# An S5 scan beside a Mish layer: row statistics of the last block on ScalarE, and another order of four w2 pairs

## The chip, the core and the metric

The kernel runs on one NeuronCore of a Trainium2 chip. The metric is the device time of one execution in microseconds (us), lower is better. TensorE (PE) multiplies matrices into PSUM banks, VectorE (DVE) and ScalarE (ACT) work element by element on SBUF and PSUM, GpSimd (POOL) and SyncE (SP) mostly issue DMAs here. Every engine works through its own list in order; where an instruction needs another engine or a DMA it waits on a semaphore, and everything behind it on that engine waits too.

## The reference

```python
x  = A_x                                   # 2048 x 1024
xn = (x - mean(x)) / sqrt(var(x) + eps)    # over the 1024 columns of each row
# A: diagonal state space model, complex
Bu = xn @ B_bar.T ;  h[t] = Lam_bar * h[t-1] + Bu[t]
yA = 2 * real(h @ Cmat.T) + xn * Dskip
# B: dense layer, F = 3584
hB = xn @ w1 + b1 ;  yB = (hB * tanh(softplus(hB))) @ w2      # Mish
out = x + yA + yB
```

## The kernel before

The 2048 rows are done in four blocks of 512 (blk 0 to 3). Each block has a first part, the products of xn with w1 (1024 x 3584) and with B, and a second, "dense 2" (Mish values times w2) followed by the product of the scanned states with C. The results of dense 2 and of C collect in the eight PSUM banks, and `finish` (L1676 in the first two blocks, L1679 in the last two) adds them to x.

In the third and fourth block (and in part in the second) the products are done by Strassen's scheme with seven products instead of eight. It needs sums of pieces of the operands. The pieces of w2 are scaled on ScalarE (`d2_row`, L1279), summed on VectorE (one `k` step is one sum, L1297), and each piece is stored by GpSimd to the scratch tensor `w2d` in HBM (`d2_store`, L1269). SyncE loads them back into the ring (`ring<-w2d`, L481), a set of seven slots of 512 KB in SBUF through which all streamed operands go to TensorE; a slot is free again when TensorE has used it. The rows of w2 go through this in five groups of two tile pairs; a group has four sums, and one semaphore counts the stores of its first three. A ring load of any of these three pieces waits for all three stores.

The Strassen products of dense 2 are called `D` (a step `D70` is product 7, first half of the rows; 10 matmuls) and `X`. Four pairs of w2 tiles go in plainly (`pl24`, `pl10`, `pl12`, `pl26`). `t0`, `t1`, `t2` and `ta0` are sums of Mish values on VectorE (L1399), `t0` for `D7`, `ta0` for `X3`. `G` steps scale Mish values on ScalarE (L938), `g` steps are Mish itself (L931), `kp` steps put PSUM results aside (L1618 on VectorE, L1624 on ScalarE).

The layer norm of the next block is made during the present one. `E` is the mean and variance of 128 rows on VectorE, `lr` the square root on ScalarE, `li` its inverse on VectorE, `ns` the normalised rows on ScalarE (L640), `tr` the transposing DMA into `xnT` (L653), `sk` and `sx` what VectorE makes from them for the next block (L647, L649, L1514). A second way stands in the code, and the second block uses it for the third: `st` (two passes on ScalarE that sum up as they go) and `nr` (root on ScalarE, two small instructions on VectorE).

```python
def ln_stats_only(blk, q):                 # E
    for h in range(2): vop(... e.bn_stats(stats[:, s, h, :], xx[...512 columns]))      # L595
    vop(... e.bn_aggr(mv[:, q, :], stats[:, s, :, :]))                                 # L597
def next_stats(blk, q):                    # st
    aop(... e.activation(xn[:, q, :], x, AF.Copy, accum_out=lnq(0, q)))                # L617
    aop(... e.activation(lnq(1, q), lnq(0, q), AF.Copy, scale=-1.0 / D))               # L619
    aop(... e.activation(xn[:, q, :], x, AF.Square, bias=lnq(1, q), accum_out=lnq(2, q)))  # L621
def next_root():                           # nr
    aop(... e.activation(ln[:, 3, :], ln[:, 2, :], AF.Sqrt, scale=1.0 / D, bias=kon[:, 2:3]))  # L625
    vop(... e.reciprocal(ln[:, 3, :], ln[:, 3, :]))                                    # L627
    vop(... e.tensor_tensor(ln[:, 4, :], ln[:, 1, :], ln[:, 3, :], op=ALU.mult))       # L628
```

The order of the work is written out by hand: one string of step names for each block (`FIRST`, `WHOLE`, `STEPS`, `LAST`), from left to right. `STEPS` is the third block. A step puts its instructions at the end of the lists of the engines that it uses. In the strings `a` to `d` with a digit are Strassen products with B, `p` to `z` those with w1, and an `e` before such a name is their evacuation from PSUM; `r` turns the states by their phases (L947, L953, L955), `sc` is a scan (L1406), `to` and `so` turn back, `al` scales the scanned states (L1650), `h16` to `h19` scale the rows of the last group of w2, `l0` loads the next x, `m4` a raw piece of w2, `Y` and `Q` are the product with C, `fin` is `finish`.

`W2_ORDER` is the order in which the first and the second block load the fourteen pairs of w2 tiles and use them in dense 2 (steps `da0` to `da27` of `WHOLE`, two for each pair). At the end of the second block's dense 2 two steps, `m2` and `m3`, load raw pieces of w2 over Mish values that are used up: `m2` first into tiles 20 to 23 of `act`, then into 24 to 27. These DMAs stand in GpSimd's list, and each waits until TensorE is done with its tiles. `h8` to `h15` scale these pieces, and four sums (`kd0`) that wait for their stores stand in VectorE's list ahead of the second block's `finish`.

Of the kernel before, what the change touches and what calls it, by code (L numbers as in the profile page):

```python
# [142 lines left out]
def bass_parallel_sum__ssm_conv_s5__dense_activation_mish__prompt_kernel(  # L143
    nc: bass.Bass,
    A_x: bass.AP,
    A_Lambda_re: bass.AP,
    A_Lambda_im: bass.AP,
    A_B_re: bass.AP,
    A_B_im: bass.AP,
    A_C_re: bass.AP,  # L150
    A_C_im: bass.AP,
    A_log_dt: bass.AP,
    A_Dskip: bass.AP,
    B_x: bass.AP,
    B_w1: bass.AP,
    B_b1: bass.AP,
    B_w2: bass.AP,
    out: bass.AP,
):
    build_kernel(nc, A_x, A_Lambda_re, A_Lambda_im, A_B_re, A_B_im, A_C_re, A_C_im,  # L160
                 A_log_dt, A_Dskip, B_w1, B_b1, B_w2, out)


def build_kernel(nc, A_x, A_Lambda_re, A_Lambda_im, A_B_re, A_B_im, A_C_re, A_C_im,
# [19 lines left out]
    GROUPS = ((0, 7), (7, NPL), (NPL, NPL + 8), (NPL + 8, NF), (12, 16), (16, 20), (20, 24), (24, 28))  # L184
    TILES = [*range(12)]
    NFG = {2: 5, 3: GF}
    W2_ORDER = tuple(range(14))
    EARLY, LATE = ((0, 20),), ((20, 28),)
    PLAIN = [(f, f + 1) for f in (24, 10, 12, 26)]
    PASSING = {}  # L190
# [19 lines left out]
    STEPS = ("p1 p5 ep1 ep5 p2 ep2 k0 k0 q1 eq1 p3 k0 q5 p6 q2 k0 ep6 eq2 s1 eq5 O0 k0 ep3 p7 es1 O0 ep7 s5 es5 k0 O0 q6 eq6 s2 es2 O0 p4 ep4 k0 q7 eq7 s6 "  # L210
# [8 lines left out]
    LAST = ("p1 ep1 p5 ep5 p2 ep2 q1 eq1 q5 eq5 p6 ep6 q2 eq2 s1 es1 p7 ep7 s5 es5 p3 ep3 q6 eq6 s2 es2 M5 p4 ep4 q7 eq7 q3 eq3 k0 k0 s6 es6 q4 eq4 g0 K0 "  # L219
# [223 lines left out]
    for blk in range(NB):  # L443
# [7 lines left out]
        else:  # L451
            items += [("w2", g) for g in W2_ORDER]
        items += [("c", j) for j in range(NJ)] if blk >= FAST else []
# [853 lines left out]
    def row_sizes(g):  # L1307
        s = (NF // 2 + g) % NRING
        for j in range(2):
            r = 2 * W2_ORDER[g] + j  # L1310
            src = ring[:, s, j * D:(j + 1) * D]
# [3 lines left out]
    def late_sizes(g, s):  # L1315
        for j in range(2):
            r = 2 * W2_ORDER[g] + j
            src = ring[:, s, j * D:(j + 1) * D].rearrange("p (d t) -> p d t", d=2)
            aop(lambda e, src=src, r=r: e.activation(CT[:, 0:2, 1, TB:D], src, AF.Abs, accum_out=wp[:, r:r + 1]),
                reads=[b_ring[s]], writes=[b_snap[0], b_wp])  # L1320
# [207 lines left out]
    def perform(blk):  # L1528
# [10 lines left out]
        for f0 in range(20, NF, 2) if blk == FAST else ():  # L1539
            left[at_item[blk, "w2", W2_ORDER[f0 // 2]]] += 1  # L1540

# [32 lines left out]
        def dense(f, us, chained=False):  # L1574
            g = (4 * REAL[f // 4] + f % 4) // 2 if split else f // 2
            at = at_item[blk, "w2", g]
            s = at % NRING
            assert n_item[0] <= at < n_loaded[0]
            wt = ring[:, s, :].rearrange("p (f d) -> p f d", f=2)
            for u in us:  # L1580
                q, h = u // 2, u % 2
                t, b_t = place(blk, f)
                opens = first[u]
                first[u] = False
                mm2(u, t[:, q * P:(q + 1) * P], wt[:, f % 2, h * TB:(h + 1) * TB], [b_t, b_ring[s]], at, opens=opens,
                    chained=chained, tell=f % 2 == 1 and u == us[-1])

        def in_order(n, us):
            dense(2 * W2_ORDER[n // 2] + n % 2, us)

        def sizes_of(g):
            at = at_item[blk, "w2", W2_ORDER[g]]
            late_sizes(g, at % NRING)
            if used(at):
                release()
# [279 lines left out]
```

## Time and profile before

| | us |
|---|---|
| median of 3 runs (lowest, highest) | 591.37 (590.75, 593.43) |
| the profiled execution | 591.81 |
| its span in the trace | 590.6 |
| TensorE busy in the span | 582.7 |
| VectorE, ScalarE, GpSimd busy | 511.2, 402.0, 151.9 |

The profiled execution took 591.81 us, 1.2 us more than its span, and lies 0.44 us above the median. Block boundaries by TensorE's first product with w1: the second block begins at about 161 us of the span, the third at 308, the fourth at 451. In the rows of the trace, the first number is the start, the second the time that a merged row takes, both in us, "xN" the number of instructions, and brackets give the idle time of the engine just before the row and what ended it.

### The profile page before, as it was taken

The page shows a single profiled execution, that of the slowest core. Times are in us where ns is not written, and L with a number is a line of the kernel's source. Part 1 is how long each engine was busy: PE and PEld are TensorE (multiplying, and loading weights), DVE is VectorE, ACT ScalarE, POOL GpSimd, SP SyncE. Part 2 cuts the span into 40 slices and gives each one's busy share as a digit, 9 for nine tenths or more (in the row PEclk, how much of TensorE's full clock was granted, in tenths as well). Part 3 has the DMA queues.
Part 4 walks back from the last instruction along what each step waited for, and adds up shares of the span by engine and source line. Part 5 has one row for each costly group of instructions (what it writes and reads, how often), then busy time and mean ns, then how long its engine had stood idle before and what let it go on. Part 6 is the DMA issues. An engine that isn't in the chain of part 4 may idle for free.

```text
span 590.6 us, 9767 instructions
## 1 busy us (share of the span) xinstructions
PE 582.7 (99%) x3631; PEld 353.0 (60%) x3631; DVE 511.2 (87%) x784; ACT 402.0 (68%) x541; POOL 151.9 (26%) x215
## 2 busy tenths in 40 slices
PE   9999999999999999999999999999999999999998
PEld 8644444444447887444448888644446888854444
DVE  6999999999796878998957789999997569789995
ACT  4859995489297778999636779976222788892330
POOL 2899200134424421332161243200000013100000
DMA  9999999999668987999999959998945946989832
GB/s 242 309 243 263 231 179 221 316 326 361 226 243 279 322 291 262 338 309 207 273 396 394 348 205 299 333 335 252 290 157 196 388 184 214 339 320 317 296 118 72
DMA packets 115369, 160.84 MB, mean 272 GB/s; under 512 B 55802, under 2 KB 66682, under 8 KB 115322
## 3 DMA queue, kind: packets, MB, share of 16 engines
q1 hardware_dynamic: 98512, 107.31, 60.6%
q0 software_dynamic: 13728, 45.62, 22.4%
q10 hardware_dynamic: 3082, 7.29, 3.4%
q8 instruction: 29, 0.48, 0.3%
q14 instruction: 18, 0.15, 0.1%
HBM read 114.05 MB, written 34.08 MB: 251 GB/s over the span
## 4 chain that ended last, share of the span: by engine, by line
PE 88%; DMA 5%; DVE 3%; ACT 3%; issue 1%; POOL 0%; DVEq 0%
PE ps L1544 44%; PE ps L1063 15%; PE ps L985 11%; PE ps L1755 10%; PE ps L1773 5%; DMA act<-in_B_w_dram 2%; DMA w2d<-act 1%; PE ps L713 1%; DMA ring<-w2d 1%; PE ps L722 1%; DMA w2d<-hb 1%; DVE xx L1676 1%; ACT act L1279 1%; ACT hb L1279 1%; PE ps L675 1%
## 5 line engine op out<-in xcount | busy, mean ns | idle before, releaser
L1544 PE MATMUL ps<-ring,act 128*128 128x512 bf16 (+1 forms) x716 | 156.2, 379 | 0.0
L1544 PEld LDWEIGHTS ps<-ring,act 128*128 128x128 bf16 (+1 forms) x716 | 70.0, 98 | 83.3 <-DMA ring<-w2d 0.2
L1544 PE MATMUL ps<-ring,hT 128*128 128x512 bf16 (+1 forms) x390 | 83.4, 376 | 0.0
L1083 ACT ACTIVATE snaps<-ps,par,cs 128x256 f32<-128x256 f32 x100 | 54.5, 562 | 40.8 <-PE ps L1063 38.5
L947 DVE TENSOR_TENSOR mt<-hT,tab 128x2048 bf16<-128x2048 bf16 (+1 forms) x56 | 68.0, 1214 | 0.4
L1544 PEld LDWEIGHTS ps<-ring,hT 128*128 128x128 bf16 x390 | 38.1, 98 | 45.0
L1406 DVE TENSOR_TENSOR_SCAN hT<-cs,qi,hT 128x512 bf16<-128x512 f32 x48 | 60.1, 1273 | 0.0
L1063 PE MATMUL ps<-TT,ring 128*128 128x256 f16 x480 | 59.8, 273 | 0.0
L1755 PE MATMUL ps<-xnT,ring 128*128 128x512 bf16 x264 | 57.3, 379 | 0.0
L1100 DVE SCALAR_TENSOR_TENSOR act<-ps,cs,snaps 128x512 bf16<-128x512 f32 x54 | 39.4, 747 | 16.0 <-PE ps L1063 13.9
L1063 PE MATMUL ps<-xnT,ring 128*128 128x256 bf16 x400 | 50.4, 273 | 1.4 <-DVE xx L1676 1.4
L1063 PEld LDWEIGHTS ps<-TT,ring 128*128 128x128 f16 (+1 forms) x480 | 46.8, 98 | 6.5
L1269 POOL DMA_DIRECT2D w2d<-hb x35 | 25.0, 716 | 87.4 <-ACT hb L1279 50.4
L1755 PEld LDWEIGHTS ps<-xnT,ring 128*128 128x128 bf16 x264 | 25.8, 98 | 31.0
L1063 PEld LDWEIGHTS ps<-xnT,ring 128*128 128x128 bf16 (+1 forms) x400 | 38.9, 98 | 6.8 <-issue 1.9
L1650 ACT ACTIVATE hT<-hT,wz 128x1024 bf16<-128x1024 bf16 x16 | 18.0, 1146 | 36.5 <-DVE hT L1646 36.5
L931 ACT ACTIVATE act<-act 128x2048 bf16<-128x2048 bf16 (+3 forms) x13 | 33.0, 2559 | 2.0 <-DVE act L1086 1.9
L1010 DVE TENSOR_TENSOR hT<-ps,snaps 128x512 f16<-128x512 f32 x36 | 23.8, 687 | 11.9 <-ACT snaps L1002 10.0
L938 ACT ACTIVATE act<-act,cs 128x512 bf16<-128x512 bf16 x48 | 30.8, 708 | 0.1
L1212 POOL DMA_DIRECT2D wsd<-hb x35 | 19.0, 546 | 42.2 <-DVE hb L1238 25.4
L1766 ACT ACTIVATE act<-ps,par 128x512 bf16<-128x512 f32 (+1 forms) x40 | 23.6, 660 | 8.2 <-PE ps L1755 8.2
L1223 ACT ACTIVATE hb<-hb,cs 128x2048 bf16<-128x2048 bf16 x10 | 19.4, 1995 | 14.1 <-DVE xx L1676 12.7
(237 smaller groups left out, 1038.2 us busy)
## 6 DMA issues: line engine op xcount, KB each, us to landing
ring<-wsd SPq DMA_DIRECT2D x110, 256.0 KB, 4.9
ring<-in_B_w_dram SPq DMA_DIRECT2D x52, 512.0 KB, 5.5
ring<-ctd SPq DMA_DIRECT2D x24, 512.0 KB, 4.6
ring<-w2d SPq DMA_DIRECT2D x24, 512.0 KB, 4.7
ring<-w2d SPq DMA_DIRECT2D x36, 256.0 KB, 4.6
wsd<-hb POOLq DMA_DIRECT2D x35, 256.0 KB, 4.8
w2d<-hb POOLq DMA_DIRECT2D x35, 256.0 KB, 5.1
hb<-in_B_w_dram POOLq DMA_DIRECT2D x20, 256.0 KB, 5.4
```

What stands on the lines that cost most here:

```text
L931: aop(lambda e: e.activation(t, t, AF.Mish), reads=b, writes=b)
L938: aop(lambda e, a=a, y=y: e.activation(a, a, AF.Copy, scale=y), reads=[b_a, b_y], writes=[b_a])
L947: vop(lambda e: e.tensor_tensor(mt[:], u.unsqueeze(1).to_broadcast([P, 2, 2, TB]), tab[:, :, j, :].unsqueeze(2).to_broadcast([P, 2, 2, TB] ...
L985: PE.mm(lambda e, w=w, x=x, o=o, begin=begin, end=end: e.matmul(ps[:, bank, o:o + TH], lhsT=w, rhs=x, start=opens and begin, stop=end, ski ...
L1063: PE.mm(lambda e, w=w, x=x, o=o, begin=begin, end=end: e.matmul(ps[:, bank, o:o + TH], lhsT=w, rhs=x, start=opens and begin, stop=end, ski ...
L1083: aop(lambda e, o=o, p=p, j=j: e.activation(o, p, AF.Identity, scale=ig, bias=b1(f0 + j)), reads=[b_ps[b], b_par, b_ig], writes=b_dst)
L1100: vop(lambda e: e.scalar_tensor_tensor(out=dst, in0=bank(b), scalar=ig, in1=src, op0=ALU.mult, op1=ALU.add), reads=[b_ps[b], b_snap[k], b_ ...
L1269: PO.dma(lambda e: e.dma_start(w2d[at // 4][:, at % 4 * TB:(at % 4 + 2) * TB].rearrange("p (j t) -> p j t", j=2), t[:, :, d, :]), sem, rea ...
L1406: vop(lambda e: e.tensor_tensor_scan(out=hT[:, ci, j, :], data0=cj("r", j).to_broadcast([P, TB]), data1=hT[:, ci, j, :], initial=init, op0 ...
L1544: PE.mm(lambda e: e.matmul(ps[:, bank, lo:hi], lhsT=lhsT, rhs=rhs, start=opens, stop=last, skip_group_check=split), reads=reads, writes=[b ...
L1755: PE.mm(lambda e, k=k, w=w: e.matmul(ps[:, bank, :], lhsT=w, rhs=xnT[:, k, :], start=k == 0, stop=k == NK - 1), reads=[b_ring[s]] + b_xnT, ...
L1773: PE.mm(lambda e, ci=ci, k=k: e.matmul(ps[:, bank + ci, :], lhsT=BT[:, ci, j, k, :], rhs=xnT[:, k, :], start=k == 0, stop=k == NK - 1), re ...
```

## The change

`W2_ORDER` becomes 0 to 9, 12, 10, 11, 13: in the first two blocks tiles 24 and 25 are used ahead of 20 to 23.

In the third block the four `E` steps, `lr0` and `li0` go, and `st0` to `st3` and `nr0` come in. Three of the `E` stood before dense 2, the fourth just after `t0`; the `st` stand among the `G` steps of dense 2 and after `kp3`, and `nr0` behind `to0`. Several neighbours change places in the same stretch.

```diff
-    W2_ORDER = tuple(range(14))
+    W2_ORDER = (*range(10), 12, 10, 11, 13)
...
-             "ec5 d5 ed5 d1 c6 k0 ed1 ec6 c3 ec3 d6 G0 ed6 G2 d3 c7 r1 ed3 ec7 l0 x1 h16 d7 ed7 x5 E1 ex1 h17 c4 h18 E0 x2 h19 ex2 ec4 k0 y5 d4 ex5 ed4 E2 "
-             "x6 ex6 y1 y2 ey1 ey5 k0 ey2 x7 x3 ex7 ex3 y6 r2 x4 ey6 k0 ex4 k0 z1 z5 ez1 G3 ez5 k0 z2 k0 y7 y3 ez2 k0 z6 z3 ez6 ey7 ez3 g2 D11 G7 ey3 y4 "
-             "k0 ey4 z7 ez7 G8 g6 G9 D10 z4 t0 D70 E3 ez4 G10 t1 kp2 t2 r3 r4 D71 D20 lr0 g7 G12 kp0 D21 r5 G4 G5 X5 li0 X6 r6 kp1 G11 kp3 pl24 ns2 pl10 "
-             "ns0 r7 ns1 G6 G13 tr0 ns3 tr1 tr2 tr3 pl12 pl26 sc20 sc00 sc21 sc50 sc01 sc10 to0 sc11 so0 al0 ta0 X3 to1 so1 sc30 al1 to2 sc41 sc31 so2 to3 "
...
+             "G1 k0 d1 c6 ec5 ed1 ec6 c3 ec3 d6 ed5 G0 ed6 d3 c7 r1 ec7 x1 ed3 h16 d7 x5 l0 h17 c4 ed7 h18 h19 ex1 x2 ex2 G2 ec4 k0 d4 ex5 y5 x6 ex6 y1 y2 "
+             "ed4 ey1 ey5 k0 x7 x3 k0 ex7 ey2 y6 ex3 r2 x4 ey6 ex4 k0 z1 k0 z5 z2 k0 ez1 y7 ez5 k0 y3 z6 ez2 G3 z3 ez6 ey7 ez3 ey3 D11 g2 G7 y4 k0 ey4 z7 "
+             "ez7 G8 D10 z4 g6 t0 D70 ez4 G9 G10 kp2 t1 D71 t2 r3 r4 D20 g7 G12 G4 D21 r5 kp0 X5 r6 G6 kp1 st1 G5 X6 G11 st2 kp3 G13 pl24 st0 sc01 sc21 "
+             "pl10 sc20 pl12 sc50 r7 sc00 st3 pl26 sc11 to0 nr0 sc10 ns1 so0 ta0 ns0 X3 to1 sc31 so1 tr0 sc30 ns3 al0 to2 ns2 sc41 al1 sc51 sc40 so2 to3 "
...
```

The lists of the engines show what this moves. First VectorE, late in the first part of the third block (one piece of the difference; L1297 are the sums of w2, L1100 and L1010 evacuations of products):

```order
-L595 BN_STATS stats<-xx 128x6 x2
-L597 BN_AGGR mv<-stats 128x2
-L595 BN_STATS stats<-xx 128x6 x2
-L597 BN_AGGR mv<-stats 128x2
-L1100 SCALAR_TENSOR_TENSOR act<-ps,cs,snaps 128x2x256
-L1297 TENSOR_TENSOR hb<-hb 128x2x512
-L595 BN_STATS stats<-xx 128x6 x2
-L597 BN_AGGR mv<-stats 128x2
-L1297 TENSOR_TENSOR hb<-hb 128x2x512
+L1100 SCALAR_TENSOR_TENSOR act<-ps,cs,snaps 128x2x256
+L1297 TENSOR_TENSOR hb<-hb 128x2x512 x3
 L1100 SCALAR_TENSOR_TENSOR act<-ps,cs,snaps 128x2x256 x3
```

The statistics are gone, and three sums instead of two stand ahead of the next three evacuations; of the five that followed these, four in a row are left, and a later single sum has moved up into that row.

Second ScalarE in dense 2, from its last group of scalings on (one piece of the difference):

```order
+L617 ACTIVATE xn,ln<-xx 128x1024
+L619 ACTIVATE ln<-ln 128x1
+L621 ACTIVATE xn,ln<-xx,ln 128x1024
 L1624 ACTIVATE KS<-ps,wz 128x512 x2
+L938 ACTIVATE act<-act,wz 128x512 x2
+L617 ACTIVATE xn,ln<-xx 128x1024
+L619 ACTIVATE ln<-ln 128x1
+L621 ACTIVATE xn,ln<-xx,ln 128x1024
+L617 ACTIVATE xn,ln<-xx 128x1024
+L619 ACTIVATE ln<-ln 128x1
+L621 ACTIVATE xn,ln<-xx,ln 128x1024
+L625 ACT_TABLE_LOAD
```

The piece begins with the second of the two `st` that now stand ahead of `kp3` (L1624); two more follow behind it, and the root with its table load comes after the last; before, two table loads and the root stood ahead of the last Mish group of the block.

Third VectorE at the end of dense 2, where the inverse root now stands (one piece of the difference):

```order
+L1406 SCALAR_TENSOR_TENSOR hT<-cs,qi,hT 128x512 x2
+L947 TENSOR_TENSOR mt<-hT,tab 128x2048
+L627 RECIPROCAL ln<-ln 128x4
+L628 TENSOR_TENSOR ln<-ln 128x4
 L1406 SCALAR_TENSOR_TENSOR hT<-cs,qi,hT 128x512
 L1644 TENSOR_TENSOR hT<-mt 128x512
```

L627 stands behind the first turn back (`to0`), one scan and `so0` ahead of `ta0`. On SyncE the four transposing DMAs go behind the first four of the eight loads of C; on GpSimd the load `m4` goes behind a second store. TensorE keeps its order but for two products with B and w1 that change places with neighbours, and but for the tiles of the new `W2_ORDER`.

6 rows, old and new, of the table STEPS are left out of this document.

## Prediction

> **What bounds the kernel now.** I read the page's first part, then TensorE's timeline for the places where it is idle, then the chain of work and each waiting engine's rows around those places. The page (engines: busy time, share, instructions):
>
> ```profile
> span 590.6 us, 9767 instructions
> PE 582.7 (99%) x3631; PEld 353.0 (60%) x3631; DVE 511.2 (87%) x784; ACT 402.0 (68%) x541; POOL 151.9 (26%) x215
> ```
>
> TensorE bounds the kernel; only 590.6 - 582.7 = 7.9 us of the span are left to win, and only where TensorE waits. Its timeline, the rows with idle time ahead of them in the part that the change touches, and the rows that date dense 2:
>
> ```profile
> 308.29 1.03 PE L1063 MATMUL ps<-xnT,ring 128*128 128x256 bf16 x8 [1.43 <-DVE xx L1676]
> ...
> 314.08 1.05 PE L1063 MATMUL ps<-TT,act 128*128 128x256 f16 x8 [1.27 <-DVE act L1238]
> ...
> 381.38 0.60 PE L1544 MATMUL ps<-ring,S 128*128 128x512 f16 x2
> 383.04 1.04 PE L1544 MATMUL ps<-ring,S 128*128 128x512 f16 x4 [1.06 <-DMA ring<-w2d]
> 384.94 3.19 PE L1544 MATMUL ps<-ring,S 128*128 128x512 f16 x14 [0.87 <-DMA ring<-w2d]
> 387.98 35.56 PE L1544 MATMUL ps<-ring,act 128*128 128x512 bf16 x164
> 423.37 27.79 PE L1544 MATMUL ps<-ring,hT 128*128 128x512 bf16 x128
> ```
>
> Two waits at the third block's start (1.43 + 1.27 = 2.70 us, on VectorE) and two in `D7` (1.06 + 0.87 = 1.93 us, on ring loads from `w2d`). Between 387.98 and the next block nothing waits: 164 matmuls fill 423.37 - 387.98 = 35.39 us, 0.216 each. The chain of work says what the waits hang on:
>
> ```profile
> 279.65 11.96 DMA act<-in_B_w_dram
> ...
> 297.07 6.91 DMA w2d<-act
> ...
> 307.01 4.53 DVE xx L1676 x4
> ...
> 373.10 0.61 DVE hb L1297
> ...
> 374.00 4.58 DMA w2d<-hb
> ...
> 378.61 6.29 DMA ring<-w2d
> 384.94 66.22 PE ps L1544 x306
> ```
>
> The first three: `m2`'s load, the stores of its pieces, the second block's `finish`. The last five: a w2 sum on VectorE, its store, the ring load that waited for it, `D7`.
>
> **The wait in D7.** SyncE's waits and issues, and its ring loads from 372 to 386 (count, size, median us to landing); then VectorE:
>
> ```profile
> SPq L481 <- DMA w2d<-hb: 4.8, 2, 3.5
> 375.61 0.32 SPq L481 DMA_DIRECT2D ring<-w2d  x1
> ...
> 381.87 0.39 SPq L481 DMA_DIRECT2D ring<-w2d  x1
> ring<-w2d SPq DMA_DIRECT2D x12, 256.0 KB, 5.5
> ```
>
> ```profile
> 363.16 1.41 DVE L595 BATCH_NORM_STATS2 stats<-xx 128x6 f32<-128x512 bf16 x2
> ...
> 365.78 2.07 DVE L1100 SCALAR_TENSOR_TENSOR act<-ps,cs,snaps 128x512 bf16<-128x512 f32 x3 [0.41 <-issue]
> ...
> 369.69 2.74 DVE L1297 TENSOR_TENSOR hb<-hb 128x1024 f16<-128x1024 bf16 x4
> ...
> 383.57 3.02 DVE L1399 TENSOR_TENSOR act<-act 128x2560 f16<-128x2560 bf16 x2 [0.16 <-ACT act L938]
> ```
>
> SyncE waited twice for stores, 3.5 and 1.3 us: at 375.61 for a group whose third sum is the first of the four at 369.69, and at 378.61 for the last group's third sum, at 373.10. Three `E` go ahead of these: at least 3 x 1.41 = 4.2 us of VectorE, by the row at 363.16. What is late next is not VectorE but the products it evacuates: the three L1100 at 365.78 keep their place behind TensorE's `x3`, so they hardly move. But the first group's third sum now stands ahead of them, with its store done long before the slot is free; its 3.5 us go. The last group's third sum becomes the fourth of the row of four instead of standing at 373.10. That row starts earlier by the 0.41 of idle time at most, at about 369.4, and the sum ends at 369.4 + 2.74 = 372.1 instead of 373.7, 1.6 earlier. Its ring load goes out at 378.61 - 1.6 = 377.0 and lands after 5.5 to 6.3 at 382.5 to 383.3; TensorE wants it at 381.38 + 6 x 0.216 = 382.7. Left: 0 to 0.6.
>
> The next in the row are the loads for `D20` behind them. The pair that holds its third unit needs the slot of the product that ends at 381.38; its second half goes out at 381.87 and by the median of 5.5 lands at 387.4. `D7` has 20 matmuls and 4 of `D20` come first: unhindered, TensorE asks for the pair at 381.38 + 24 x 0.216 = 386.6, where today it asks at 387.98 + 0.86 = 388.8. So up to 0.8 (1.6 if it takes the 6.29 of the row above) of the gain turns into a new wait there. The four loads ahead of it are spread over more time, so I take 0.5: a gain of 1.93 - 0.5 = **1.4 us**, ends 0.3 (a 1.6 wait left) and 1.93.
>
> The fourth `E` costs nothing today: the two `t1`, `t2` sums at 383.57 waited for ScalarE's L938, so VectorE would only have waited longer. Its removal gains nothing. `h16` to `h19` moved together, `m4` one store later, the two products that changed places: bounded by the same waits, 0, since TensorE had no wait between 314.08 and 381.38.
>
> **The new statistics.** ScalarE's rows (the second block's `st`, two starts of it; then dense 2):
>
> ```profile
> 241.69 1.04 ACT L617 ACTIVATE xn<-xx 128x1024 bf16<-128x1024 bf16 x1
> ...
> 244.25 1.04 ACT L617 ACTIVATE xn<-xx 128x1024 bf16<-128x1024 bf16 x1
> ...
> 381.00 2.54 ACT L938 ACTIVATE act<-act,cs 128x512 bf16<-128x512 bf16 x4
> ...
> 384.71 1.28 ACT L632 ACT_TABLE_LOAD   x1
> 386.00 0.30 ACT L632 ACTIVATE ln<-mv,kon 128x4 f32<-128x4 f32 x1
> ...
> 387.61 1.91 ACT L931 ACTIVATE act<-act 128x2048 bf16<-128x2048 bf16 x1
> ...
> 400.91 1.27 ACT L1624 ACTIVATE KS<-ps,wz 128x512 f32<-128x512 f32 x2 [6.35 <-PE ps L1544]
> ```
>
> One `st` takes 244.25 - 241.69 = 2.56 us. Without the root and its two loads, Mish starts at 384.7 instead of 387.61 and ends at 386.6; then five scaling pairs of 1.25 (2.54 for four instructions) and two `st`: 386.6 + 6.2 + 5.1 = 397.9. That fills the 6.35 us in which ScalarE waited for `X6`. `kp3` follows when `X6` ends, 400.9 - 1.4 = 399.5, and takes 1.2; then a scaling pair, two `st`, the load and the root: 399.5 + 1.2 + 1.25 + 5.1 + 1.28 + 0.3 = **408.6**.
>
> VectorE waits for that root at L627, and behind it stand a scan, `so0`, `ta0`, all turns and scans, and the third block's `finish`:
>
> ```profile
> 408.04 1.28 DVE L1406 TENSOR_TENSOR_SCAN hT<-cs,qi,hT 128x512 bf16<-128x512 f32 x1
> ...
> 409.89 1.48 DVE L1399 TENSOR_TENSOR act<-act 128x2560 f16<-128x2560 bf16 x1
> ...
> 446.02 1.28 DVE L1679 SCALAR_TENSOR_TENSOR xx<-ps,wz,KS 128x1024 bf16<-128x1024 f32 x1 [1.22 <-PE ps L1544]
> ```
>
> Up to L627 VectorE does what it did up to 408.04 (less `li0`, 0.3), so it comes there at about 407.7 and waits 0.9. With 0.3 for its two small instructions, 1.85 (409.89 - 408.04) for scan and `so0`, and 1.48, `ta0` ends at 408.6 + 0.3 + 1.85 + 1.48 = 412.2 instead of 411.4. TensorE reaches `X3` 40 matmuls ahead of 423.37, at 414.7, with the gain at 413.3. Margin 1.1: cost 0. `finish` had 1.22 us to spare, less 0.8 later and 1.4 earlier wanted: it runs 1.0 late against TensorE; but the fourth block's first product needs its first bank only 451.0 - 447.3 = 3.7 after it, so 0. I bound this term by 0 and 2 (root two or more us late, less margin).
>
> The Trainium skill, "ScalarE: Activation LUTs", section "What ACT_TABLE_LOAD costs", gives 1283 ns for the load and some 1380 ns more of drain at every switch. In the rows above the root starts 0.01 after a load of 1.28, with no such gap. By the page the root would come at 410.0, `ta0` would eat the margin and X3 would wait 0.3: 590.8 instead of the 590.5 below.
>
> The transposing DMAs wait on SyncE for the fourth slot of C, by TensorE's pace some 418 instead of 409; the sums that read `xnT` stand just ahead of `finish` at 446. That leaves over 20 us: 0.
>
> **The new w2 order.** In the second block tiles 20 to 23 are now done two tiles later. `m2`'s first load, which GpSimd issued as soon as tile 23 was done, waits 16 x 0.216 = 3.45 us longer; its second load waits for tile 27 as before. GpSimd's rows, the first load's size and time to land, and what GpSimd's queue moved in 273:276, 276:279 and 288:291 (packets, MB, share):
>
> ```profile
> 272.62 0.72 POOL L1264 DMA_DIRECT2D act<-in_B_w_dram  x1 [1.93 <-PE ps L1544]
> 279.65 2.14 POOL L1264 DMA_DIRECT2D act<-in_B_w_dram  x3 [6.32 <-PE ps L1544]
> act<-in_B_w_dram POOLq DMA_DIRECT2D x1, 512.0 KB, 10.5
> q0 software_dynamic: 7, 0.02, 7.9%
> q0 software_dynamic: 80, 0.31, 82.8%
> q0 software_dynamic: 131, 0.50, 44.0%
> ```
>
> Both loads must land before `h8`, at 291.6, and from there the chain above runs to TensorE without slack: `finish` is late already, TensorE waits 2.70. A load later by s costs s. In its first 3.4 us the load moved 0.02 MB, the next three 0.31. If all 0.31 are pushed behind 288, they take 0.31 / 0.50 x 3 = 1.9 us there; if the queue moves them a little later beside the same transposing DMAs, almost nothing. Ends: 3.45 lost (the whole wait) and, if the transposes get done sooner without it, 2.70 won. Nearest are the rows of its slow start: I take **0.5 us lost**. The first block only loads rows of B 3.45 later, in VectorE's and ScalarE's slack there: 0.
>
> **Sum.** 591.81 - 1.4 + 0.5 + 0 = 590.9 for the profiled execution, which lies 0.44 above the median: **590.5**, 0.9 less than before (0.15%). A change of this kernel under 0.5% (3.0 us) can hardly be told from none.
>
> **Rivals.**
> - Nothing won: the gain ends in the loads of `D20`, which need the slot freed at 381.38, and the rest in `m2`. 591.4. For it: the slot's date does not move. Against it: even the slowest of these loads leaves 0.3, and a load lost to `m2` must cost the rest.
> - Slower by `m2`: the 3.45 us are passed on whole. From 1.4 on, it decides the sign. 591.37 - 1.4 + 3.45 = 593.4. For it: the chain there has no slack. Against: 0.02 MB in the first 3.4 us.
> - Slower by the root: each 1 us after 409.7 at which L627 is released delays `X3` by 1 us, and after 411.1 the kernel is slower than with no change. Two `st` of 3.6 instead of 2.56 behind `kp3` would do that. 591.37 + 1 = 592.4.
> - Both waits shrink: `m2` lands sooner since the transposes are not shared with; up to 1.4 + 2.0: 588.0. For it only that engine time was held by the transposes.
>
> **How the numbers follow.** Forecast 0.52 (590.5, its own range 589.6 to 591.1), nothing won 0.22 (591.4), `m2` 0.12 (593.4), root 0.07 (592.4), both 0.07 (588.0). The range for 8 in 10 leaves out the farther half of "both" and most of the `m2` case: 588.8 to 592.8. Faster by over 0.5% (under 588.4) only in half of "both" and little else: 0.06; slower (over 594.3) by an `m2` load that costs more than 3.45 or a root late as well: 0.05; the rest 0.89.
>
> **What would show it.** The waits in `D7` on ring loads fall from 1.93 to 0.6 or less, a wait of 0 to 1 us appears some 5 us on, at `D20`. ScalarE has no idle time ahead of `kp3`; VectorE waits about 0.9 for ScalarE at L627, and no row of TensorE waits at `X3`. The two waits near 308 grow together by about 0.5. I am wrong if TensorE waits for L1399 at `X3`, for a product's evacuation around 362 to 367 (ScalarE's list is tight there, with `h16` to `h19` ahead), or if the waits near 308 change by more than 2.

## The result, and the profile after

The changed kernel takes 588.78 us (median of 9 runs, 587.50 to 589.71); the kernel before, timed beside it, 592.47 (9 runs, 590.29 to 596.26). The ratio is 0.9933, interval 0.9906 to 0.9959: 0.67% faster, where 0.15% was forecast. The profiled execution took 588.81 us with a span of 587.5. Two very slow runs do not enter the ratios further down: one of the kernel before at 1030.73 us, which is left out of the counts too, and one at 597.15 with the third block's steps alone.

```profile
span 587.5 us, 9776 instructions
PE 582.2 (99%) x3631; PEld 352.0 (60%) x3631; DVE 507.3 (86%) x772; ACT 411.1 (70%) x561; POOL 151.8 (26%) x215
```

The span is 3.1 us shorter (590.6 before). TensorE's timeline, its rows from the third block's start to the end of dense 2 that have idle time in brackets, and the two that stood at 308.29 and 314.08 before:

```profile
307.24 1.04 PE L1063 MATMUL ps<-xnT,ring 128*128 128x256 bf16 x8
...
311.61 1.04 PE L1063 MATMUL ps<-TT,act 128*128 128x256 f16 x8
...
378.89 4.48 PE L1544 MATMUL ps<-ring,S 128*128 128x512 f16 x20
...
385.30 1.02 PE L1544 MATMUL ps<-ring,act 128*128 128x512 bf16 x4 [1.06 <-DMA ring<-w2d]
386.62 33.84 PE L1544 MATMUL ps<-ring,act 128*128 128x512 bf16 x156 [0.30 <-DMA ring<-w2d]
420.30 27.79 PE L1544 MATMUL ps<-ring,hT 128*128 128x512 bf16 x128
```

Both waits at the third block's start are gone: 1.43 + 1.27 = 2.70 us. The 20 matmuls of `D7` (the row at 378.89) run without a wait, and `D20` behind them waits 1.06 + 0.30 = 1.36 instead of the 1.93 in `D7`: 0.57 less. Together 3.27 between the two profiles, of which the rest of the program gives back 0.2. So most of it comes from the place where I expected a loss of 0.5: `m2`. GpSimd's rows there, then ScalarE's first `h` step and VectorE's `kd0` and `finish`:

```profile
276.63 0.72 POOL L1264 DMA_DIRECT2D act<-in_B_w_dram  x1 [5.39 <-PE ps L1544]
280.20 2.14 POOL L1264 DMA_DIRECT2D act<-in_B_w_dram  x3 [2.86 <-PE ps L1544]
```

```profile
287.95 8.42 ACT L1279 ACTIVATE act<-act,cs 128x1024 bf16<-128x1024 bf16 x8 [0.49 <-DMA act<-in_B_w_dram]
```

```profile
298.59 2.94 DVE L1297 TENSOR_TENSOR act<-act 128x1024 f16<-128x1024 bf16 x4 [1.06 <-DMA w2d<-act]
302.27 1.22 DVE L1676 TENSOR_TENSOR xx<-ps,xx 128x1024 bf16<-128x1024 f32 x1 [0.74 <-PE ps L1544]
```

The same two steps before:

```profile
291.63 4.27 ACT L1279 ACTIVATE act<-act,cs 128x1024 bf16<-128x1024 bf16 x4 [4.72 <-DMA act<-in_B_w_dram]
```

```profile
304.06 2.94 DVE L1297 TENSOR_TENSOR act<-act 128x1024 f16<-128x1024 bf16 x4 [7.10 <-DMA w2d<-act]
```

The first load goes out 4.0 us later (276.63 against 272.62), and yet the data are there 3.7 us earlier (287.95 against 291.63). `kd0` starts at 298.59 instead of 304.06, and `finish` now waits for TensorE, not TensorE for `finish`. What the DMAs did in that stretch, in windows of 4 us (DMA share and GB/s are the last two columns), before:

```profile
276.00:280.00 4.00, 4.00 (x20) 1.83 (x19) 1.92 (x13) 3.88 (x7) 0.35 (x1) 1.00 1.20 139
280.00:284.00 4.00, 4.00 (x20) 1.78 (x19) 3.59 (x16) 4.00 (x3) 1.79 (x3) 1.00 0.99 187
284.00:288.00 4.00, 4.00 (x20) 1.84 (x19) 3.90 (x7) 2.91 (x2) 0.00 (x0) 1.00 1.02 119
```

and after:

```profile
276.00:280.00 4.00, 4.00 (x20) 1.80 (x19) 2.17 (x12) 3.85 (x9) 0.72 (x1) 1.00 1.12 210
280.00:284.00 4.00, 4.00 (x20) 1.82 (x19) 3.48 (x18) 4.00 (x3) 2.14 (x3) 1.00 1.06 365
284.00:288.00 4.00, 4.00 (x20) 1.79 (x19) 3.93 (x6) 3.51 (x3) 0.00 (x0) 1.00 1.03 394
```

The share is the same, about 1, in both: the DMA engines were occupied, but moved under half as much over these 12 us (a third in the last four). The four transposing DMAs of the third block's x, all on SyncE (time from issue to landing), before:

```profile
L653 SPq DMA_TRANSPOSE xnT<-xn x4: 1237/1237/1594, 262.5 to 274.9; - x4
...
DMA to landing us min/median/max: 4.3/7.7/14.0
```

and after:

```profile
L653 SPq DMA_TRANSPOSE xnT<-xn x4: 1237/1281/1420, 263.0 to 275.5; - x4
...
DMA to landing us min/median/max: 4.3/5.0/5.7
```

The slowest took 14.0 us before and 5.7 after. Before, the third transpose was issued 0.07 us ahead of `m2`'s first load (272.62); SyncE's row:

```profile
272.55 1.24 SPq L653 DMA_TRANSPOSE xnT<-xn  x1
```

Both then crawled, and so did what followed them. I call this the clash; that the two going out together is what brings it on is so far only an argument, which the experiments test.

### The profile page after: what moved, and what is told of

It reads as the page before. It is cut to its first block, busy times and chain, and to the rows that moved or that the text cites. A ratio compares the mean times of both kernels' runs of the same rounds, so it can differ in the third digit from the quotient of the medians.

```text
span 587.5 us, 9776 instructions
## 1 busy us (share of the span) xinstructions
PE 582.2 (99%) x3631; PEld 352.0 (60%) x3631; DVE 507.3 (86%) x772; ACT 411.1 (70%) x561; POOL 151.8 (26%) x215
## 4 chain that ended last, share of the span: by engine, by line
PE 96%; DMA 2%; SPq 1%; issue 0%; DVE 0%
PE ps L1544 49%; PE ps L1063 19%; PE ps L985 12%; PE ps L1755 10%; PE ps L1773 5%; DMA ring<-in_B_w_dram 1%; PE ps L722 1%; DMA ring<-w2d 1%; PE ps L713 0%; SPq L428 0%; SPq L481 0%; PE ps L547 0%; SPq L489 0%; SPq L432 0%; DVE xx L1709 0%
## 5 line engine op out<-in xcount | busy, mean ns | idle before, releaser
L1100 DVE SCALAR_TENSOR_TENSOR act<-ps,cs,snaps 128x512 bf16<-128x512 f32 x54 | 39.5, 747 | 20.8 <-PE ps L1063 16.6
L1010 DVE TENSOR_TENSOR hT<-ps,snaps 128x512 f16<-128x512 f32 x36 | 23.9, 687 | 10.0 <-ACT snaps L1002 8.0
L1773 PE MATMUL ps<-xnT,BT 128*128 128x512 bf16 x128 | 27.8, 379 | 0.0
```

The source lines that it names most:

```text
L1100: vop(lambda e: e.scalar_tensor_tensor(out=dst, in0=bank(b), scalar=ig, in1=src, op0=ALU.mult, op1=ALU.add), reads=[b_ps[b], b_snap[k], b_ ...
L1773: PE.mm(lambda e, ci=ci, k=k: e.matmul(ps[:, bank + ci, :], lhsT=BT[:, ci, j, k, :], rhs=xnT[:, k, :], start=k == 0, stop=k == NK - 1), re ...
```

## The experiments

"Over 590" below counts timed runs of a kernel above 590 us. The times of `before` have no gap there (589.79, 589.90 and 590.05 are among them); the line is drawn by the profiles. Leaving out the one with the extra `st`, the five profiled executions with the clash took 590.57 to 592.46 us, the eight without it 587.52 to 589.30.

**The w2 order alone.** `before` with one line:

```diff
-    W2_ORDER = tuple(range(14))
+    W2_ORDER = (*range(10), 12, 10, 11, 13)
```

> The kernel before with the new w2 order alone. Theory C (clash): the first load of m2 used to go out between two of the transposing DMAs, and both became slow; 3.45 us later it goes out behind them. Then the four transposes land within 6 us each (14.0 the slowest before), m2 and m3 within 11 (15.4 before), the two waits near 308 fall from 2.70 to under 0.3, and the waits in D7 stay near 1.9: 2.7 less than before, a ratio of 0.9955. Rival S (the gain comes from the third block's steps): the waits near 308 stay at 2.7, ratio 1.000. My prediction's term (0.5 lost): 1.001.

Ratio 0.9973 (0.9948 to 0.9997), median 588.49, 12 runs between 587.42 and 589.70. Its profile has no wait near 308; transposes within 5.8 us, `m2` and `m3` within 11.3. This is what theory C expected of the waits and transfers. The ratio is less far from 1 than expected because the kernel before was often as fast on this chip: 35 runs from 587.49 to 596.17, 16 of them over 590, the other 19 with a median of 588.29. The new order brings no faster executions; it takes the slower ones away.

**The third block's steps alone.** The changed kernel with the old order:

```diff
-    W2_ORDER = (*range(10), 12, 10, 11, 13)
+    W2_ORDER = tuple(range(14))
```

> The changed kernel with the old w2 order, so the third block's steps alone. Theory C: the waits near 308 are 2.5 to 2.9 as before, the slowest transpose lands after about 14 us, and of D7's 1.93 about 1.4 is left at D20: 0.6 less than before, a ratio of 0.999. Rival S: the waits near 308 are gone here too, ratio 0.994. By my prediction's term for D7 (1.4 won): 0.9975.

Ratio 1.0003 (0.9963 to 1.0044): 5 of 12 runs over 590, the other 7 with a median of 588.26, as with the kernel before. The profiled execution took 592.46; its transposes and `m2`'s loads, and TensorE at the third block's start:

```profile
DMA to landing us min/median/max: 4.3/8.4/14.9
...
DMA to landing us min/median/max: 11.3/14.4/17.7
```

```profile
309.74 1.27 PE L1063 MATMUL ps<-xnT,ring 128*128 128x256 bf16 x8 [2.75 <-DVE xx L1676]
```

The clash is back with the old order, and with it the wait. Rival S falls.

This execution lost time in a second way. Right behind the wait of 2.75 us the granted TensorE clock was 0.60 (310 to 312 us) and 0.55 (312 to 314), and the row above took 1.27 us instead of 1.03. In the other four profiles with the clash, whose wait at this place was 1.21 to 2.42 us, the clock stayed at 1.00. The mean clock of a whole run was 0.997 here; it lies below 1.000 in 13 of the 35 runs of `before` over 590 in the three later comparisons and in no run of any kernel under 590. So a part of what the slowest runs lose is probably this lower clock; only this one trace shows it at work.

**The load's date without the tile order.** `before` with `m2`'s halves swapped, in `d2_load`:

```diff
-        for h in range(2):
+        for h in ((1, 0) if g == 2 else (0, 1)):
```

> The kernel before, w2 order and all, but m2 loads its second half (tiles 24 to 27) first; since GpSimd works in order, the load into tiles 20 to 23 then also goes out only after tile 27, near 280, 7 us later than before. Theory C: without a load between the transposes these land within 6 us, all four loads of m2 and m3 within 12, and the waits near 308 fall to under 1: ratio 0.9955 to 0.998. Rival O (the order of the tiles itself helps, not the date of the load): the waits stay at 2.7 or grow. My prediction's reasoning (a later load costs what it is late): 3.45 to 7 us slower, ratio 1.006 to 1.012.

Ratio 0.9972 (0.9945 to 0.9998), 12 runs between 587.52 and 589.25; transposes within 5.1 us, loads within 10.9, no wait near 308. A load 7 us later costs nothing here, and the order of the tiles is not needed: my price for lateness and rival O both fall.

**Where must the load stand to the transposes?** In the changed kernel both late transposes moved back, then (second experiment) only the third, next to the fourth:

```diff
-             "da19 tr1 ... da20 da21 ls10 tr2 da22 da23 ls11 tr3 da24 da25 ls12 da26 da27 ls13 ..."
+             "da19 tr1 ... da20 da21 ls10 da22 da23 ls11 tr2 da24 da25 ls12 tr3 da26 da27 ls13 ..."   # first
+             "da19 tr1 ... da20 da21 ls10 da22 da23 ls11 tr2 tr3 da24 da25 ls12 da26 da27 ls13 ..."   # second
```

> The changed kernel with the third and fourth transposing DMA each moved behind the next load of C on SyncE (about 2.4 us later), so that m2's first load at 276.6 goes out between them again, as it did before the change. Theory C: a transpose needs over 8 us again, m2's loads 11 or more, and the waits near 308 come back with 1 to 2.7 us: against the kernel before a ratio of 0.996 to 0.999. Rival O (order of the tiles) or a theory in which only the load's own date counts: the waits stay near 0, ratio 0.9935 as the changed kernel.

> The changed kernel with the third transposing DMA moved directly ahead of the fourth (both from about 275.5, the fourth at about 276.8), so that m2's first load at 276.6 is issued while SyncE issues them; in the kernel before, the load went out 0.07 us after the third transpose began to issue, in the experiment with later transposes 1.1 us after it and no clash followed. Theory C3 (the clash needs a load that is issued together with a transpose): part of the runs lie over 590 again, a third to a half as with the old order, and a profile there shows a transpose over 8 us. Theory C1 (the load must go out well ahead of the last transposes, as in the kernel before, with two transposes still to come): no or one run over 590, as with the changed kernel.

Neither brought the clash back: 0.9974 (0.9947 to 1.0002) with 1 of 12 runs over 590, and 0.9961 (0.9937 to 0.9984) with none; transposes within 6.4 and 5.8 us. So theory C in its first form is too wide: a load that goes out about 1 us behind one transpose and ahead of the next does no harm. C3 as stated for the second experiment missed as well; there the load went out 1.1 us behind the start of the third transpose and about 0.2 ahead of that of the fourth.

**The same moves in the kernel before**, whose load stays at 272.6: both late, only the third, only the fourth:

```diff
-             "... ls10 tr2 da22 da23 ls11 tr3 da24 da25 ls12 da26 da27 ls13 ..."
+             "... ls10 da22 da23 ls11 tr2 da24 da25 ls12 tr3 da26 da27 ls13 ..."   # both
+             "... ls10 da22 da23 ls11 tr2 tr3 da24 da25 ls12 da26 da27 ls13 ..."   # third
+             "... ls10 tr2 da22 da23 ls11 da24 da25 ls12 tr3 da26 da27 ls13 ..."   # fourth
```

> The kernel before, old w2 order, with the third and fourth transposing DMA each behind the next load of C on SyncE: issued near 275 and 277.4, with m2's first load at 272.6 ahead of both, by 2.4 us instead of 0.07 behind the third's start. Theory C3 (only issue at the same time clashes): no run over 590, as fast as the changed kernel, ratio 0.997. Theory C1 (a load in flight while two transposes run clashes, whenever it was issued): a third to a half of the runs over 590, ratio 1.000.

> The kernel before with only the third transposing DMA moved, behind the next load of C and directly ahead of the fourth (issued near 275 instead of 272.5); m2's first load stays at 272.6 and is then 2.4 us ahead of both. Theory C3a (the clash needs the third transpose issued together with the load): no run over 590, no transpose over 6 us, ratio about 0.996. Theory C4 (it needs the fourth transpose, about 2.3 us behind the load): a third to a half of the runs over 590, a transpose of about 14 us in a profile there, ratio 1.000.

> The kernel before with only the fourth transposing DMA moved, behind the next load of C (issued near 277.4 instead of 275); the third still goes out at the same time as m2's first load, 272.5 and 272.6. Theory C3a (third transpose and load together): a third to a half of the runs over 590, as before, ratio 1.000. Theory C4 (fourth transpose 2.3 us behind the load): no run over 590, ratio about 0.996.

| moved in `before` | ratio (interval) | over 590 | `before` beside it |
|---|---|---|---|
| both | 0.9962 (0.9938 to 0.9985) | 0 of 12 | 12 of 23 |
| third | 0.9977 (0.9952 to 1.0002) | 1 of 12 | 7 of 22 |
| fourth | 1.0060 (1.0028 to 1.0092) | 10 of 12 | 7 of 22 |

As long as the third transpose goes out together with the load, the runs over 590 stay; there are even more of them than C3a expected, and why is open. Move that transpose by 2.4 us and they all but go (0 and 1 of 12, transposes within 5.6 us in both profiles), with the w2 order and the load as they were. The third alone would not be clear of noise, since its interval reaches 1.0002; the three experiments together are. The profile with only the fourth moved fell on one of the two quick executions, 588.43 us. SyncE, GpSimd and the transposes in it, then the same windows as above:

```profile
272.17 1.42 SPq L653 DMA_TRANSPOSE xnT<-xn  x1
```

```profile
272.21 0.72 POOL L1264 DMA_DIRECT2D act<-in_B_w_dram  x1 [1.90 <-PE ps L1544]
```

```profile
DMA to landing us min/median/max: 4.1/5.3/5.9
```

```profile
276.00:280.00 4.00, 4.00 (x21) 1.81 (x19) 1.92 (x13) 3.88 (x7) 0.76 (x2) 1.00 1.08 345
280.00:284.00 4.00, 4.00 (x20) 1.81 (x19) 3.63 (x13) 4.00 (x3) 1.38 (x2) 1.00 1.12 297
284.00:288.00 4.00, 4.00 (x20) 1.83 (x19) 3.90 (x7) 3.74 (x4) 0.00 (x0) 1.00 1.01 387
```

Issued within 0.04 us of each other, yet nothing clashed here: being together makes the clash possible, not certain. VectorE, ScalarE and GpSimd have nearly the same work in these windows as in the kernel before (from 276 to 280 us 1.92, 3.88 and 0.76 us busy here, 1.92, 3.88 and 0.35 there), so their work does not tell the two apart.

**The kernel before, profiled twice more.**

> The kernel before once more, for a second profile of it: its runs on this chip lie in two groups, 587.5 to 589.8 and 590 to 596. Theory C2 (the clash happens in part of the executions, and is what parts the two groups): a profile of an execution under 589.8 shows four transposes within 6 us, m2's loads within 11, some 300 GB/s or more between 280 and 288 and no wait near 308; one over 590 shows a transpose of about 14 us, 100 to 200 GB/s there and waits of 2 to 5 us near 308. Rival (the groups have another cause, such as the start or D7): an execution under 589.8 with the slow transpose too, or one over 590 without it.

> As the run just ahead of it, a third profile of the kernel before: under 589.8 with transposes within 6 us, or over 590 with one of about 14 us, by theory C2.

590.57 and 590.64 us, both with the clash; the first:

```profile
308.42 1.03 PE L1063 MATMUL ps<-xnT,ring 128*128 128x256 bf16 x8 [1.70 <-DVE xx L1676]
314.22 1.05 PE L1063 MATMUL ps<-TT,act 128*128 128x256 f16 x8 [1.27 <-DVE act L1238]
383.48 3.19 PE L1544 MATMUL ps<-ring,S 128*128 128x512 f16 x14 [0.51 <-DMA ring<-w2d]
```

The slowest transpose took 13.5 and 14.4 us. No execution of `before` under 590 has been profiled, so for that half of C2 the quick execution above has to stand. These profiles gave something else: the wait in `D7`, 1.93 us in the profile that I predicted from, is 0.51 and 0.70 here.

**One more `st`.** `sc00 st3` became `sc00 st3 st3` in the changed kernel.

> The changed kernel with the statistics of the last 128 rows made twice (st3 st3), so that the root comes one st (2.56 us) later. By the prediction's term for the root: L627 then waits 2.0 + 2.6 = 4.6 us instead of 2.0, ta0 ends 2.6 later, and since it ended about 1.0 ahead of X3 in the changed kernel, TensorE waits about 1.6 us at X3 for L1399. Rival (the margin is not what the rows say, something else releases X3 or the wait is made up): no wait, or the whole 2.6.

592.78 us, one run. VectorE and TensorE:

```profile
411.27 0.18 DVE L627 RECIPROCAL ln<-ln 128x4 f32<-128x4 f32 x1 [4.70 <-ACT ln L625]
```

```profile
414.95 8.81 PE L1544 MATMUL ps<-ring,act 128*128 128x512 bf16 x40 [1.60 <-DVE act L1399]
```

As expected, 1.60 at `X3`. (The rest of its time lies in waits elsewhere, 1.17 at `D20` and 1.10 near 361; the second comes up again below.)

**Without three E.** `E1`, `E0` and `E2` taken out of `STEPS` of the kernel before.

> The kernel before without its first three E steps: it leaves out the mean and variance of 384 of the last block's rows and uses old values for them; nothing else is moved. By the prediction's step for D7 VectorE's sums come up to 1.6 us earlier than before at the last group, SyncE waits less for stores, the wait in D7 falls from 1.93 to 0.6 or less, and a wait of 0.5 to 1.4 appears at D20 for the slot that z4 sets free; together 0.5 to 1.9. Rival (the neighbours' new order did it, not the missing E): D7 keeps 1.5 or more. The waits near 308 stay 2.7 in both.

592.11 us, one run, with the clash (2.42 + 1.28 near 308). TensorE in `D7` and `D20`:

```profile
384.52 3.19 PE L1544 MATMUL ps<-ring,S 128*128 128x512 f16 x14 [0.51 <-DMA ring<-w2d]
389.98 33.84 PE L1544 MATMUL ps<-ring,act 128*128 128x512 bf16 x154 [0.54 <-DMA ring<-w2d]
```

Inside what was expected, but it decides nothing: the kernel before, with its `E`, has 0.51 and 0.70 in the other two profiles.

## Why the prediction was wrong, point by point

- **The m2 term is the step that failed.** The sum had 0.5 lost, between 2.70 won and 3.45 lost; 2.70 was won between the two profiles. I treated the load as one piece of a chain, where later means later, and its slow start as queueing. It was one of two parties to a clash that slowed the transposes and every load behind them. The rows to see it stood in the prediction: in 276:279 GpSimd's queue moved 0.31 MB in 82.8% of 3 us, 125 GB/s while busy; in 288:291 0.50 MB in 44.0%, 379 GB/s. I read the megabytes and not the megabytes per share. The rival "both waits shrink" (588.0, chance 0.07) had the mechanism for these waits, at too small a chance. What inside the DMA engines makes the two slow each other stays open.
- **The time before was not one number.** All 9 runs of `before` timed with the change lie over 590 (the three that I started from are among them), but in the three later comparisons only 16 of 35, 12 of 23 and 7 of 22, the others near 588.3 to 588.6. Why the first comparison has none under 590 is open. The change takes the runs over 590 away (none of 9; with the order alone none of 12) and leaves the others where they were. It was itself timed only this once, at 0.67%; its w2 order alone gave 0.27% where 16 of 35 runs of `before` were over 590, so the gain to expect hangs on how often the clash falls. The range, 588.8 to 592.8, missed the median by 0.02; of the 3.7 us between the medians, 1.1 is only that the nine runs of `before` have a higher median than the first three.
- **The D7 term was over-sized.** Forecast 1.4 won (0.3 to 1.93), measured 0.57 between the two profiles, in the way described: SyncE waited once for stores, until 376.69 (377.0 forecast), `D7` was freed, and a new wait came at `D20` behind the slot that `z4` frees. The 0.5 left there became 1.36: the pair's last load took 6.13 us (380.45 to 386.58) and not the median 5.5, and with 6.13 the prediction's own sum gives 1.4. But even 0.57 is not shown to be the change's. In the five profiles with the new steps `D7` never waits and `D20` always does, 0.23 to 1.36 in all; in the nine with the old steps `D7` always waits, and the two places together cost 0.51 to 1.93; the mean is 0.9 in both. The steps alone measure 1.0003 (0.9963 to 1.0044), too wide to tell 0.6 us (0.1%) from none. The 1.93 was the high end of what differs from execution to execution.

The chain of work after shows the pair's load:

```profile
380.45 6.13 DMA ring<-w2d
...
386.62 5.57 PE ps L1544 x25
```

- **The statistics were right.** Cost 0 was forecast, and no row of TensorE waits at `X3`. ScalarE and VectorE around the root:

```profile
397.84 1.26 ACT L1624 ACTIVATE KS<-ps,wz 128x512 f32<-128x512 f32 x2 [2.47 <-PE ps L1544]
...
405.44 1.28 ACT L625 ACT_TABLE_LOAD   x1
406.73 0.30 ACT L625 ACTIVATE ln<-ln,kon 128x4 f32<-128x4 f32 x1
```

```profile
407.06 0.18 DVE L627 RECIPROCAL ln<-ln 128x4 f32<-128x4 f32 x1 [2.01 <-ACT ln L625]
...
409.20 1.48 DVE L1399 TENSOR_TENSOR act<-act 128x2560 f16<-128x2560 bf16 x1
```

From `kp3` to the root's end I had 408.6 - 399.5 = 9.1; it is 407.03 - 397.84 = 9.2. `ta0` ends at 410.68, `X3` starts 40 matmuls ahead of 420.30, at 411.66: a margin of 0.98 against the forecast 1.1, and the extra `st` bears it out (L627 waited 4.70 - 2.01 = 2.69 longer, X3 1.60: 1.09 of margin). Two details missed: ScalarE still had 2.47 us idle ahead of `kp3`, which I had called filled although my own sum left 399.5 - 397.9 = 1.6, and VectorE waited 2.01 for the root and not 0.9, because its scans came earlier. The Trainium skill, "ScalarE: Activation LUTs", section "What ACT_TABLE_LOAD costs", adds some 1380 ns of drain to a load. Here, too, the root starts 0.01 after its load of 1.28, so the trace does not bear it out.
- **Of the slower rivals**, `root` kept its margin, and `m2` had the right place and the wrong sign. The products' evacuation around 362 to 367, named as a way to be wrong, made no wait in the profile of the changed kernel. But it did in two of the five profiles with the new steps: 1.10 us with the extra `st` and 1.01 with the transposes together. In the nine with the old steps TensorE waits for ScalarE nowhere there. ScalarE and TensorE with the extra `st`, whose list is the changed kernel's up to there:

```profile
354.84 4.27 ACT L1279 ACTIVATE hb<-hb,cs 128x1024 bf16<-128x1024 bf16 x4 [1.71 <-DMA hb<-in_B_w_dram]
```

```profile
360.30 1.03 PE L1063 MATMUL ps<-TT,ring 128*128 128x256 f16 x8 [0.44 <-ACT snaps L1083]
361.99 1.91 PE L1063 MATMUL ps<-xnT,ring 128*128 128x256 bf16 x16 [0.66 <-ACT hT L1029]
```

The first row is `h16` to `h19`. Moved together they start 3.1 us earlier than before (353.15 in the profile after, 356.27 before), while the load of the piece that they scale goes out when it did (345.29, 345.55). When it lands late, they wait for it (1.71 us here, 1.62 in the other), and the evacuations behind them come late. The prediction put this move at 0 because TensorE had no wait there before; a move can bring one that was not there.
- **Slips in the working.** The forecast's own range, 589.6 to 591.1, is not what its terms give: with 0.5 lost to `m2`, 1.93 and 0.3 won make 589.9 and 591.6. The root's line at 411.1 leaves that 0.5 out (410.6 with it), and two `st` of 3.6 behind `kp3` put the root at 410.7 and the time at 591.5, not 592.4. Neither changes what failed.

## What to carry to other kernels

Where the DMA share stays near 1 and the same stretch moves two or three times as much in another execution or another version, ask which transfers meet there. A low rate alone is no sign: between 60 and 80 us the changed kernel moves 222 GB/s at a share of 1.06. Moving one party, here a transpose by 2.4 us or the load by 4 or 7, took away waits of 2.7 us without making anything shorter; price a transfer's date by whom it meets, not only by when it ends. Take the spread of the runs for a reading as well: a wait of 2.7 us in one profile can belong to half of the executions, and a gain computed from it to half of them too. "Nothing waits there now" prices a move at 0 only if the move brings no instruction closer to what it waits for. A term that rests on one wait of a ring load (here 0.51 to 1.93 in three profiles of one kernel) needs more than one profile.

## What the runs showed of the hardware

A plain 512 KB load issued by GpSimd within 0.07 us of a transposing DMA issued by SyncE can drop the traffic of the core to 99 to 256 GB/s between 280 and 288 us (five profiles, the slowest transpose 13.5 to 14.9 us), against 297 to 401 in eight profiles without the clash (slowest transpose within 6.4 us; a ninth, with the extra `st`, has one of 8.0, 238 GB/s from 280 to 284, and no wait near 308). The Trainium skill, "DMA: Bandwidth & Descriptors", section "Rules for kernel authors", says that a transpose next to ordinary DMAs needs nothing. It says so of keeping transfers apart so that the data come out right, and gives no time; in these rows such a neighbour cost time. What parts the executions that clash from those that don't stays open: the load followed the transpose by 0.06 to 0.07 us in the five with the clash and by 0.04 in the one without, and a shift of less than 1 us against the third transpose was not tried.
